# Batch 1's scores from interleaved queries, with its transposes inside batch 0's chain and batch 0's values loaded and transposed earlier

## The chip, the cores and the metric

The kernel runs on one core of a Trainium2 chip. The metric is device time in microseconds (us) of one execution. The runs of the kernel before have a median of 314.97 us over 14 runs (lowest 314.67, highest 319.38). One further execution was recorded by the hardware profiler; it took 315.0 us, and the span that the profile describes is 313.2 us of it.

The engines are named as in the profile: PE is the matrix engine, PEld its weight loads, DVE the vector engine, ACT the scalar engine, POOL the GpSimd engine, SP the sync engine. [...]

## The reference

Two computations follow one another. The first is an attention with a local window and eight global positions (8 batches, 8 heads, 576 positions, 64 numbers a head):

```python
scores = scale * np.matmul(q, k.transpose(0, 1, 3, 2))
mask = np.abs(pos[:, None] - pos[None, :]) <= 32
mask = mask | is_global[:, None] | is_global[None, :]
scores = np.where(mask, scores, -1000000000.0)
attn = softmax(scores)
x = attn @ v                    # then heads side by side: [8, 576, 512]
```

The second mixes along positions and then along channels:

```python
h = np.maximum(x^T @ w_tok1, 0) @ w_tok2     # 576 -> 256 -> 576
u = x + h^T
out = u + np.maximum(u @ w_ch1, 0) @ w_ch2   # 512 -> 1536 -> 512
```

## The kernel before

**Tiles and stages.** A batch has 576 positions: four tiles of 128 and a last one of 64. Its eight heads are two groups (`hg`) of four. Its stages are these.

- Load. `load_qk` and `load_v` issue DMAs from POOL's queue. Queries and keys land with positions on the partitions; `Xk` and `Xq` (L239 to L249) are DVE transposes of 32x32 blocks that bring the head dimension to the partitions, into the staging buffers `kcs[hg]` and `qcs[hg]`. `Kc` and `Xc` (L257 to L265) copy from there into `kT` and `qT`, whose tiles carry the eight global positions beside each tile's own (interleaved). `globals_` and `globals_k` write the global columns.
- Values. `V = vsh[b % 2]` has eight chunks `c`. `load_v(b)` issues a DMA for each; `dup_v(b)`, an SP DMA, then fills partitions 32 to 127 of chunks 5 to 7 with a copy of chunks 2 to 4. Batch 0 is different: `load_v0` brings the values of its middle positions into `v16` with four DMAs, `Xv0` transposes them on DVE (two halves, L142), and `shift_v0` copies on DVE (L134) what `dup_v` copies elsewhere.
- Scores (`S_...`): for a head group and one of two parts, matmuls with 32 rows write up to 512 columns for each head into PSUM, and `S_exp` (L323) lets ACT write the exponentials to `e_all` (`e0` for batch 0). The mask is either a bias that extra matmuls add (`biasm`, L298), or a multiplication by `bandm` afterwards on DVE (`S_mask`, L342). `S_eg` (L348) collects the global rows.
- `OG` (L358, and `OGh` L590 for batch 0) is the output of the global rows. Its result is written into the first rows of `V` (L364, L368), and a function `rest` (L371) copies it to further chunks.
- `PV` (L390, L393) multiplies with the values, and `norm` (L401, L402) divides on DVE.
- `M1` and `M2` are the mixing along positions, `M3` a transpose, `M4` (L472) and `M5` (L498) the mixing along channels: `M4` of a batch is 12 units of four matmuls of 512 columns, `M5` 16 units of three.

**Order.** Everything is one program written out in order; there is no scheduler. Batches from 1 on run as a software pipeline, in the loop at L1024: while the matrix engine does `M4` and `M5` of batch b, the scores of batch b+2 and the output stage of batch b+1 are woven in by `merge`. The head of the program does not have that. From L829 on batch 0 runs alone as a chain, one head group after another: scores, `OGh`, `rfh`, `PVh`, `normh`, `M1h`, `M2h`, `M3h`, `M4h`. After it, in the loop's turn `b == 0`, an order written out by hand (L1034 to L1040) runs the scores of batch 1 (`T`), its `OG` and `PV`, the preparation of batch 2 (`x2`) and the `M4` units of batch 0 (`M[2]` to `M[11]`) together. `M1(1)` ends it, and `M5` of batch 0 with the scores of batch 2 follows.

**Batch 1's scores.** In the kernel before they go through `S_nat` (L291), as batch 0's do: queries are read from `qcs[hg]` in plain order, so a stretch of columns that holds global positions too is cut into pieces by `pieces`, and the global columns come from `gqT` with matmuls of 8 columns. All four tiles of head group 1 carry the bias; those of head group 0 are masked on DVE. A tile here is two heads (`rp`) of a group and part. From batch 2 on, `S_mm` (L280, L286) reads the interleaved `qT` instead, four heads together.

**Buffers.** The PSUM pools are: `pss`, two buffers of two banks; `psv`, one buffer of two banks; `psm`, two of one bank. Score tiles take `pss` (some of batch 0's take `psv`).

Of the kernel before, what the change touches and what calls it, by code (L numbers as in the profile page):

```python
# [17 lines left out]
P = 128  # L18
NT = 5
# [6 lines left out]
NC = 8  # L26
# [26 lines left out]
def kernel(  # L53
# [12 lines left out]
    nc = tc.nc  # L66
# [65 lines left out]
    def shift_v0():  # L132
        for p in (32, 64):
            nc.vector.tensor_copy(  # L134
                out=vsh[0][p + 32 : p + 64, NT:NC].rearrange("p c h x -> p c (h x)"),
                in_=vsh[0][p : p + 32, 2:NT].rearrange("p c h x -> p c (h x)"),
            )

    def Xv0():
        for half in range(2):  # L140
# [173 lines left out]

    def S_exp(b, hg, part, rp, ps):
# [37 lines left out]
    def OG(b, get):  # L353
# [16 lines left out]
        def rest():  # L370
            (nc.vector.tensor_copy if b > 1 else nc.scalar.copy)(  # L371
# [362 lines left out]
    def zero_e(e):  # L734
        zeros(e[:, :, 136:208])
        zeros(win(e[:, :, 408:440], EB, 3))
# [87 lines left out]
    load_v0((0, 1))  # L824
    gather(gk, k, 0, (1,))
    gather(gq, q, 0, (1,))
    load_v0((2, 3))
# [12 lines left out]
    zero_e(e_all)  # L840
# [25 lines left out]
    nc.vector.memset(vsh[0][32:64, NT:NC, :, 0:D], 0.0)  # L866
# [12 lines left out]
    Xq(0, 1)  # L879
    glob0(1)  # L880
    S_nat(0, 0, 1, 0, psv, True)
    S_nat(0, 0, 1, 1, pss, True)
    load_v(0, (0, 5, 6, 7), False)
# [10 lines left out]
    load_v(1, range(NC), False)  # L894
    dup_v(1)
    S_nat(0, 1, 0, 0, pss, True)
    S_nat(0, 1, 0, 1, psv, True)
    Xv0()
    shift_v0()
    nc.vector.memset(e0[:, 0:4, 200:208], 0.0)  # L900
    S_eg(0, 0)

# [11 lines left out]
    S_nat(0, 1, 1, 1, pss, True)  # L914
    rfh(0, og)
# [49 lines left out]
    M3e(0, 0, pu[:, 0], nc.scalar.copy)  # L965
    Xk(1, 0)
    M2e(1, 0, h1[:, 0], False)
# [9 lines left out]
    M4h(1, (0, 1), 0, 4)  # L977
    M4h(0, (2, 3), 0, 2)
# [3 lines left out]
    load_qk(2, (0,))  # L982
    load_wc2()
    load_qk(2, (1,))
    load_v(2)

    def S1(hg, part, rp):
        S_nat(1, hg, part, rp, pss, hg == 1)

    globals_k(1, nc.vector, 1)  # L990
    Kc(1, 0, nc.vector)
    globals_k(1, nc.vector, 0, slice(0, 1))
    Xq(1, 0)
    Xk(1, 1)
    Kc(1, 1, nc.vector)
    globals_k(1, nc.vector, 0, slice(1, 2))
    Xq(1, 1)
# [26 lines left out]
    for b in range(B):  # L1024
        D4, D5 = dense(b)
        if b == 0:
            T = lambda *a: S1(*a)
            M = [f for _, f in D4]
            og, *pv = [f for _, f in phase_og(1)]
            x2 = []  # L1030
            for hg in range(2):
                x2.append(lambda hg=hg: (Xk(2, hg), Kc(2, hg, nc.vector), globals_k(2, nc.vector, 0, slice(hg, hg + 1))))
                x2.append(lambda hg=hg: Xq(2, hg))
            for f in (  # L1034
                lambda: M2(0, 2, psv), lambda: T(0, 0, 0), M[2], lambda: T(0, 0, 1), M[3], lambda: T(0, 1, 0), lambda: T(0, 1, 1), M[4],
# [59 lines left out]
```

## Time and profile before

| | |
|---|---|
| profiled execution | 315.0 us |
| its span in the profile | 313.2 us |
| median of 14 runs | 314.97 us |
| PE busy | 297.1 us, 95% |
| DVE busy | 191.2 us, 61% |
| ACT busy | 158.8 us, 51% |
| POOL busy | 106.1 us, 34% |
| chain that ended last, by engine | PE 77%, DVE 12%, issue 3%, ACT 3%, POOL 2%, DMA 1% |

Places on the span, in us from its start: batch 0's first scores at 11.05; its first `OGh` at 21.28; its first `M4h` at 36.56; batch 1's first scores at 38.9; batch 1's `OG` at 53.96; `M1(1)` from 61.39 to 63.71; first `M5` of batch 0 at 63.55; `M4` of batch 1 at 79.79.

A busy share is an average over stages. Durations in a row of groups are means of one instruction. Times of PE are those of the record, and neighbouring matmuls overlap. "Idle before" tells how long the engine was idle before an instruction and, behind the arrow, what ended the wait; "issue" there means that the engine waited for nothing that the profile shows.

### The profile page before, as it was taken

The page shows a single profiled execution, that of the slowest core. Times are in us where ns is not written, and L with a number is a line of the kernel's source. Part 1 is how long each engine was busy: PE and PEld are TensorE (multiplying, and loading weights), DVE is VectorE, ACT ScalarE, POOL GpSimd, SP SyncE. Part 2 cuts the span into 40 slices and gives each one's busy share as a digit, 9 for nine tenths or more (in the row PEclk, how much of TensorE's full clock was granted, in tenths as well). Part 3 has the DMA queues.
Part 4 walks back from the last instruction along what each step waited for, and adds up shares of the span by engine and source line. Part 5 has one row for each costly group of instructions (what it writes and reads, how often), then busy time and mean ns, then how long its engine had stood idle before and what let it go on. Part 6 is the DMA issues. An engine that isn't in the chain of part 4 may idle for free.

```text
span 313.2 us, 8382 instructions
## 1 busy us (share of the span) xinstructions
PE 297.1 (95%) x3507; PEld 161.8 (52%) x3507; DVE 191.2 (61%) x368; ACT 158.8 (51%) x321; POOL 106.1 (34%) x203
## 2 busy tenths in 40 slices
PE   8979897899989999999999999999999999999994
PEld 3668674544456445544466446444565446444641
DVE  8966785867556685947573867776582866240021
ACT  8964596666335454465446535563546625205500
POOL 7995282300688074217412371408030000000000
PEclk9998999999999999999999999999999999999999
DMA  7999999917699799628990499329601720061022
GB/s 108 129 120 195 194 143 222 154 42 150 130 143 159 134 126 150 161 47 122 137 183 0 70 143 209 86 70 135 132 2 16 154 69 2 0 167 50 3 86 82
DMA packets 69494, 34.66 MB, mean 111 GB/s; under 512 B 55984, under 2 KB 59952, under 8 KB 69456
## 3 DMA queue, kind: packets, MB, share of 16 engines
q0 software_dynamic: 44960, 18.19, 49.8%
q1 hardware_dynamic: 24496, 15.94, 20.5%
q8 instruction: 27, 0.44, 0.6%
q14 instruction: 11, 0.09, 0.1%
HBM read 36.38 MB, written 9.44 MB: 146 GB/s over the span
## 4 chain that ended last, share of the span: by engine, by line
PE 77%; DVE 12%; issue 3%; ACT 3%; POOL 2%; DMA 1%; DVEq 0%; ACTq 0%
PE b1p L472 25%; PE op L498 23%; PE a1p L415 5%; DVE e_all L342 5%; PE hp L431 4%; PE s L286 4%; PE b1lp L485 3%; PE pv L390 3%; PE s L309 2%; PE pv L393 2%; DMA v<-in_v_dram 1%; PE og L358 1%; DVE osb L502 1%; ACT e_all L323 1%; DVE u L436 1%
## 5 line engine op out<-in xcount | busy, mean ns | idle before, releaser
L699 ACT ACTIVATE big<-b1p 128x512 f16<-128x512 f32 x96 | 57.2, 598 | 79.3 <-PE b1p L472 78.0
L472 PE MATMUL b1p<-uT,wc 128*128 128x512 f16 x376 | 91.9, 379 | 2.6 <-DVE osb L502 1.5
L498 PE MATMUL op<-big 128*128 128x512 f16 x384 | 91.8, 380 | 0.0
L323 ACT ACTIVATE e_all<-s 128x544 f16<-128x544 f32 (+3 forms) x140 | 58.8, 515 | 34.1 <-PE s L286 30.8
L498 PEld LDWEIGHTS <-big 128*128 128x128 f16 x384 | 35.5, 98 | 40.5
L472 PEld LDWEIGHTS <-wc 128*128 128x128 f16 x376 | 33.3, 97 | 39.3 <-issue 6.5
L125 POOL DMA_DIRECT2D vsh<-in_v_dram x60 | 41.8, 709 | 20.4 <-DMA wc<-in_moe_w_ch_dram 5.4
L342 DVE TENSOR_TENSOR e_all<-e_all,bandm 128x1160 f16<-128x1160 f16 x52 | 36.7, 757 | 14.6 <-ACT e_all L323 14.6
L502 DVE TENSOR_TENSOR osb<-u,op 128x512 f32<-128x512 f16 x32 | 21.9, 684 | 24.3 <-PE op L498 24.0
L436 DVE TENSOR_TENSOR u<-x,hp 128x1024 f16<-128x1024 f16 x14 | 17.1, 1218 | 30.6 <-PE hp L431 30.6
L348 POOL COPY eg<-e_all 128x160 f16<-128x160 f16 (+1 forms) x24 | 6.4, 295 | 77.9 <-DVE e_all L342 77.9
L402 DVE TENSOR_TENSOR x<-pv,rr 128x512 f16<-128x512 f32 (+1 forms) x35 | 24.2, 691 | 1.3
L253 POOL COPY kT<-kc 128x640 int32<-128x640 int32 x11 | 8.1, 733 | 40.5 <-DVE rr L401 35.0
L390 PEld LDWEIGHTS <-e_all 128*128 128x128 f16 (+1 forms) x280 | 18.1, 98 | 6.4 <-issue 2.0
L390 PE MATMUL pv<-vsh,e_all 128*128 128x66 f16 (+1 forms) x280 | 20.3, 193 | 0.2 <-DVE x L402 0.2
L431 PE MATMUL hp<-a,w 128*128 128x512 f16 x72 | 19.1, 379 | 0.9 <-DVE u L436 0.9
L240 DVE STREAM_TRANSPOSE kc<-k 128x576 int32<-128x576 int32 x16 | 19.9, 1242 | 0.1
L246 DVE STREAM_TRANSPOSE qc<-q 128x576 int32<-128x576 int32 x16 | 19.8, 1239 | 0.0
L393 PE MATMUL pv<-vsh,e_all 128*128 128x66 f16 x224 | 17.2, 193 | 0.6 <-DVE vsh L368 0.6
L286 PEld LDWEIGHTS <-kT 32*128 32x128 f16 x768 | 11.9, 92 | 10.7 <-issue 9.9
L364 DVE TENSOR_TENSOR vsh<-og,dsel 32x132 f16<-32x132 f32 x28 | 8.1, 289 | 13.7 <-PE og L358 13.3
L393 PEld LDWEIGHTS <-e_all 128*128 128x128 f16 x224 | 14.6, 97 | 3.1
(161 smaller groups left out, 339.3 us busy)
## 6 DMA issues: line engine op xcount, KB each, us to landing
out_dram<-osb SPq DMA_DIRECT2D x32, 256.0 KB, 2.3
k<-in_k_dram POOLq DMA_DIRECT2D x16, 288.0 KB
q<-in_q_dram POOLq DMA_DIRECT2D x16, 288.0 KB
vsh<-in_v_dram POOLq DMA_DIRECT2D x36, 96.0 KB
vsh<-vsh SPq DMA_DIRECT2D x7, 297.0 KB, 5.7
wc<-in_moe_w_ch_dram POOLq DMA_DIRECT2D x3, 512.0 KB
big<-in_moe_w_ch_dram POOLq DMA_DIRECT2D x3, 512.0 KB
out_dram<-osb SPq DMA_DIRECT2D x8, 128.0 KB, 7.8
```

Source lines behind the costliest of these rows:

```text
L125: nc.gpsimd.dma_start(out=V[p0:p1, c, :, 0:D], in_=v[b, :, j0 : j0 + p1 - p0, :].rearrange("h p d -> p h d"))
L286: nc.tensor.matmul(tiles[r // 2][:, r % 2, off : off + n], lhsT=kT[rs, kc : kc + P, e], rhs=qf[rs, lo : lo + n, e], start=(e == 0), stop=( ...
L323: nc.scalar.activation(out=o, in_=i, func=AF.Exp, scale=scale)
L342: nc.vector.tensor_mul(out=eh, in0=eh, in1=bandm)
L390: nc.tensor.matmul(o[0:m], lhsT=e[:, h, c0 : c0 + m], rhs=vs[:, tau, h, :], start=True, stop=(tau == NT - 1))
L393: nc.tensor.matmul(o, lhsT=e[:, h, c1 : c1 + P], rhs=vs[:, NT - 1 + tau if tau else 1, h, :], start=False, stop=True)
L402: nc.vector.tensor_tensor(out=x16[r, tau, :].rearrange("p (f h x) -> p f h x", f=2, h=4), in0=pq[r, :, :, 0:D], in1=rr[r].unsqueeze(3).to_ ...
L431: nc.tensor.matmul(ps[:, i, :], lhsT=w2[:, ch, P * tau - sh : P * tau - sh + P], rhs=s["a1"][:, ch, :], start=(ch == 0), stop=(ch == 1),)
L472: nc.tensor.matmul(ps, lhsT=wc1[:, cc, P * j : P * j + P], rhs=s["uT"][:, :, cc, :], start=(cc == 0), stop=(cc == 3))
L498: nc.tensor.matmul(ps, lhsT=w, rhs=wc2[:, j, :], start=(j == 0), stop=(j == NJ - 1))
L502: nc.vector.tensor_add(out=osb, in0=s["u16"][:, tau], in1=ps)
L699: nc.scalar.activation(out=st[b]["b1"][:, j, :], in_=ps, func=AF.Relu)
```

## The change

**Values of batch 0.** All four `load_v0` DMAs are issued before the two gathers of head group 1 (before: two ahead of them and two behind), and `load_v(0, (0,))` directly after these, ahead of POOL's copy `Kc(0, 1)`. `Xv0` is split into its two halves, which stand around `glob0(1)` on DVE, ahead of six score tiles; before, both stood behind these, just ahead of `shift_v0`. The memset of a part of `vsh[0]` moves from DVE to ACT. The zeroing of `e_all`, which stood there on ACT, moves behind batch 0's last score tile.

**Batch 1's keys and queries.** `Xq(1, 0)` joins `Xk(1, 0)` inside batch 0's chain, and the four transposes of batch 1 are all ahead of its first score tile. `Kc(1, ...)` goes from DVE to POOL. `Xc(1, ...)`, which did not exist for batch 1, is added on POOL. `globals_(1)` (which did not exist either) and `globals_k(1, ..., 1)` run on DVE at about the place of batch 0's first `S_eg`.

**Batch 1's scores.** A new function `S_tile` takes the place of `S_nat`: the same tile of two heads, read from `qT` in uncut stretches. Only two of the eight tiles keep the bias (`hg == 1 and rp == 1`), and `S_mask(1, 1, (0, 1))` is added on DVE. The first tile is issued between batch 0's `M4h` groups.

**Values of batch 1.** The loads are issued in another order, in between other work on POOL. `dup_v(1)` is replaced by the DVE copies (`shift_v(1)`) and a memset on POOL. `rest` of batch 1 goes from ACT to DVE.

**Preparation of batch 2.** Its `Kc` and `Xc` go to POOL (before: `Kc` twice and `Xc` once on DVE, `Xc` once on ACT). `load_v(2)` is split: three chunks at the old place, and five with `dup_v(2)` at the end of the written-out order.

The diff, cut to its core:

```diff
-    def shift_v0():
+    def shift_v(b):
...
-    def Xv0():
-        for half in range(2):
+    def Xv0(half):
+        if True:
...
+    def S_tile(b, hg, part, rp, bias):
+        ps = pss([P, 2, 512], name=f"s_{b}_{hg}_{part}_{rp}")
+        qf, kT = q16s[b % 2][:, hg], k16s[b % 2][:, hg]
+        if bias:
+            for i in range(2):
+                for off, c0, n in B_SEG[part]:
+                    nc.tensor.matmul(
+                        ps[:, i, off : off + n], lhsT=identS, rhs=biasm[:, c0 : c0 + n], start=(off == 0), stop=False,
+                    )
+        for off, kc, lo, n in S_SEG[part]:
+            for e in range(2):
+                for i in range(2):
+                    r = 2 * rp + i
+                    rs = slice(32 * r, 32 * r + 32)
+                    nc.tensor.matmul(
+                        ps[:, i, off : off + n], lhsT=kT[rs, kc : kc + P, e], rhs=qf[rs, lo : lo + n, e],
+                        start=(e == 0 and not bias), stop=(e == 1 and (off == S_SEG[part][-1][0] or not bias)),
+                    )
+        S_exp(b, hg, part, rp, ps)
...
         def rest():
-            (nc.vector.tensor_copy if b > 1 else nc.scalar.copy)(
+            nc.vector.tensor_copy(
...
-    load_v0((0, 1))
+    load_v0((0, 1, 2, 3))
     gather(gk, k, 0, (1,))
     gather(gq, q, 0, (1,))
-    load_v0((2, 3))
+    load_v(0, (0,), False)
...
-    zero_e(e_all)
+    zeros(vsh[0][32:64, NT:NC, :, 0:D])
...
-    nc.vector.memset(vsh[0][32:64, NT:NC, :, 0:D], 0.0)
     glob0(0)
...
     Xq(0, 1)
+    Xv0(0)
     glob0(1)
+    Xv0(1)
     S_nat(0, 0, 1, 0, psv, True)
     S_nat(0, 0, 1, 1, pss, True)
-    load_v(0, (0, 5, 6, 7), False)
+    load_v(0, (5, 6, 7), False)
...
     eg_const(1, nc.gpsimd.tensor_copy)
-    load_v(1, range(NC), False)
-    dup_v(1)
+    nc.gpsimd.memset(vsh[1][32:64, NT:NC, :, 0:D], 0.0)
+    load_v(1, (2, 3, 4), False)
     S_nat(0, 1, 0, 0, pss, True)
     S_nat(0, 1, 0, 1, psv, True)
-    Xv0()
-    shift_v0()
+    shift_v(0)
     nc.vector.memset(e0[:, 0:4, 200:208], 0.0)
     S_eg(0, 0)
+    globals_(1, nc.vector)
+    globals_k(1, nc.vector, 1)
...
     S_nat(0, 1, 1, 1, pss, True)
+    zero_e(e_all)
     rfh(0, og)
...
     M3e(0, 0, pu[:, 0], nc.scalar.copy)
+    load_v(1, range(1), False)
     Xk(1, 0)
+    Kc(1, 0, nc.gpsimd)
+    Xq(1, 0)
+    Xc(1, 0, nc.gpsimd)
+    load_v(1, range(1, 2), False)
     M2e(1, 0, h1[:, 0], False)
...
     M4h(1, (0, 1), 0, 4)
+    globals_k(1, nc.vector, 0, slice(0, 1))
+    Xk(1, 1)
+    Kc(1, 1, nc.gpsimd)
+    Xq(1, 1)
+    Xc(1, 1, nc.gpsimd)
+    globals_k(1, nc.vector, 0, slice(1, 2))
+    load_v(1, range(5, 8), False)
+    load_qk(2, (0,))
+    load_wc2()
+    load_qk(2, (1,))
+    load_v(2, range(3), False)
+
+    def S1(hg, part, rp):
+        S_tile(1, hg, part, rp, hg == 1 and rp == 1)
+
+    S1(0, 0, 0)
     M4h(0, (2, 3), 0, 2)
...
-    load_qk(2, (0,))
-    load_wc2()
-    load_qk(2, (1,))
-    load_v(2)
-
-    def S1(hg, part, rp):
-        S_nat(1, hg, part, rp, pss, hg == 1)
-
-    globals_k(1, nc.vector, 1)
-    Kc(1, 0, nc.vector)
-    globals_k(1, nc.vector, 0, slice(0, 1))
-    Xq(1, 0)
-    Xk(1, 1)
-    Kc(1, 1, nc.vector)
-    globals_k(1, nc.vector, 0, slice(1, 2))
-    Xq(1, 1)
...
-            og, *pv = [f for _, f in phase_og(1)]
+            _, *pv = [f for _, f in phase_og(1)]
+            og = lambda: OG(1, pss)()
             x2 = []
+            gk2 = [lambda hg=hg: globals_k(2, nc.vector, 0, slice(hg, hg + 1)) for hg in range(2)]
             for hg in range(2):
-                x2.append(lambda hg=hg: (Xk(2, hg), Kc(2, hg, nc.vector), globals_k(2, nc.vector, 0, slice(hg, hg + 1))))
-                x2.append(lambda hg=hg: Xq(2, hg))
+                x2.append(lambda hg=hg: (Xk(2, hg), Kc(2, hg, nc.gpsimd)))
+                x2.append(lambda hg=hg: (Xq(2, hg), Xc(2, hg, nc.gpsimd)))
             for f in (
-                lambda: M2(0, 2, psv), lambda: T(0, 0, 0), M[2], lambda: T(0, 0, 1), M[3], lambda: T(0, 1, 0), lambda: T(0, 1, 1), M[4],
-                lambda: T(1, 0, 0), lambda: S_mask(1, 0, (0, 1)), lambda: T(1, 0, 1), lambda: S_mask(1, 0, (2, 3)), lambda: S_eg(1, 0),
-                M[5], lambda: T(1, 1, 0), lambda: globals_k(2, nc.vector, 1), x2[0], lambda: T(1, 1, 1), M[6], lambda: nc.vector.memset(e_all[:, 4:8, 200:208], 0.0),
-                lambda: S_eg(1, 1), x2[1], M[7], og, M[8], pv[0], lambda: globals_(2, nc.vector), pv[1], M[9], pv[2], pv[3], M[10], pv[4], lambda: Xc(2, 0, nc.scalar), x2[2], M[11],
-                lambda: M1(1, pss), x2[3], lambda: Xc(2, 1, nc.vector),
+                lambda: T(0, 0, 1), lambda: M2(0, 2, psv), M[2], lambda: T(0, 1, 0), M[3], lambda: T(0, 1, 1),
+                lambda: S_mask(1, 0, (0, 1)), lambda: T(1, 0, 0), lambda: S_mask(1, 0, (2, 3)), lambda: S_eg(1, 0), M[4],
+                lambda: T(1, 0, 1), lambda: T(1, 1, 0), M[5], lambda: T(1, 1, 1), lambda: shift_v(1), lambda: S_mask(1, 1, (0, 1)),
+                lambda: nc.vector.memset(e_all[:, 6:8, 200:208], 0.0), lambda: S_eg(1, 1), lambda: globals_k(2, nc.vector, 1), M[6], M[7], x2[0], og, M[8], M[9], pv[0], pv[1],
+                lambda: globals_(2, nc.vector), pv[2], x2[1], M[10], pv[3], pv[4], M[11], lambda: M1(1, pss), gk2[0],
+                x2[2], x2[3], gk2[1], lambda: load_v(2, range(3, 8)),
             ):
                 run(f)
```

## The prediction

> **What bounds the kernel now.** I read the page's first part, then the stretches of ten microseconds, then the chain of waits of the head, then PE's timeline and the groups by shape. The page, and the table of stretches (busy time and count of each engine, TensorE clock, DMA share, GB/s):
>
> ```profile
> PE 297.1 (95%) x3507; PEld 161.8 (52%) x3507; DVE 191.2 (61%) x368; ACT 158.8 (51%) x321; POOL 106.1 (34%) x203
> ```
>
> ```profile
> 10.00:20.00 10.00, 8.83 (x258) 7.35 (x256) 7.80 (x19) 9.51 (x20) 9.35 (x15) 1.00 0.93 98
> 20.00:30.00 10.00, 8.36 (x217) 7.13 (x218) 6.74 (x22) 5.09 (x12) 7.34 (x12) 0.83 1.13 177
> 30.00:40.00 10.00, 8.89 (x111) 6.53 (x108) 7.72 (x14) 5.22 (x10) 3.11 (x5) 1.00 1.49 193
> 40.00:50.00 10.00, 9.86 (x254) 7.02 (x253) 8.41 (x20) 9.13 (x22) 6.95 (x11) 1.00 1.24 173
> 50.00:60.00 10.00, 7.59 (x140) 4.85 (x140) 6.00 (x18) 4.90 (x8) 3.08 (x5) 1.00 1.46 195
> 100.00:110.00 10.00, 10.00 (x135) 4.86 (x133) 5.07 (x7) 5.01 (x12) 1.19 (x4) 1.00 0.82 154
> ```
>
> From about 64 us on PE is full; the change leaves that alone. It works on the head, where no engine is full throughout: ACT is at 9.1 of 10 from 40 to 50, PE loses 2.4 from 50 to 60, the clock is down from 20 to 30. So what was late in each part decides. The chain of waits, head (start, length, what):
>
> ```profile
> 13.24 4.20 DMA v<-in_v_dram
> ...
> 17.52 2.13 DVE vsh L142 x2
> ...
> 19.68 0.56 DVE vsh L134
> ...
> 21.28 0.43 PE og L590 x25
> ...
> 49.86 1.70 issue
> ...
> 55.90 0.30 DVE vsh L368
> ```
>
> Batch 0's values set the time of its first `OGh`: DMA, transpose, shift. Much later PE stands still for 1.70 in the middle of a score tile, waiting for nothing that the record names. PE's timeline at the two gaps, and ACT in between (its idle time before):
>
> ```profile
> 21.28 0.43 PE L590 MATMUL og<-vsh,eg 128*32 128x66 f16 x32 [1.83 <-DVE eg L348]
> ```
>
> ```profile
> 49.12 1.03 ACT L323 ACTIVATE e_all<-s 128x544 f16<-128x544 f32 x2 [0.45 <-PE s L309]
> 52.24 1.03 ACT L323 ACTIVATE e_all<-s 128x544 f16<-128x544 f32 x2 [2.09 <-PE s L309]
> ```
>
> Last, POOL's timeline where it waits for a free place in its DMA queue, which tells when earlier loads landed, and PE's row of a four-head score step:
>
> ```profile
> 30.87 0.77 POOL L125 DMA_DIRECT2D vsh<-in_v_dram x1 [1.59 <-DMA wc<-in_moe_w_ch_dram]
> ...
> 57.87 0.58 POOL L125 DMA_DIRECT2D vsh<-in_v_dram x1 [0.83 <-DMA k<-in_k_dram]
> 59.63 0.58 POOL L125 DMA_DIRECT2D vsh<-in_v_dram x1 [1.18 <-DMA q<-in_q_dram]
> ```
>
> ```profile
> 68.43 0.62 PE L286 MATMUL s<-qT,kT 32*128 32x136 f16 x32
> ```
>
> [...] an instruction block of 16 KB is among the DMA packets from 49.3 to 50.2, where the stall begins (49.86), with the data queues full (DMA share 1.24). [...] Here 0.83 over ten microseconds is 3.4 us at half, right after the 1.83 gap. [...] POOL copies of 0.72 to 0.75 from 97.6 to 100.9 stand beside transposes of 1.19 that are no longer than others (1.25); beside DVE copies no run here shows them.
>
> **Part by part.**
>
> *1. Values of batch 0.* The third and fourth `load_v0` move past two gathers on POOL (1.02 + 0.99 + two pauses of 0.30): issued by 11.3 instead of 13.88, landing near 17.44 - 2.6 = 14.8. DVE is 0.91 early (memset 0.70 and its pause 0.21 gone), so `Xq(0,1)` ends near 14.45. `Xv0(0)` 14.8 to 15.9. The gathers go 1.26 later, the query one from 12.66 to 13.9; before, its data were there at 15.64 without a wait; I take 16.0. `glob0(1)`, 0.63, to 16.6; `Xv0(1)` to 17.7; two shifts, 1.14, to 18.9; `S_eg` to 19.3. `OGh` at 19.4 or, with pauses, 19.7 instead of 21.28: 1.6 (0.5 if the gather lands at 17). `Kc(0,1)` goes 0.7 later, to 15.5, hidden: its reader starts after 16.8. ACT's 1.40 of zeroing is replaced by one of 1536 columns, near 1.45 by the slope of its rows (576 in 0.67, 768 in 0.83).
>
> The gap on PE falls from 1.83 to some 0.6, and with it the reason of the half clock. What that cost: a biased tile 1.96 instead of 1.22 (by the chain's rows), 32 `PVh` matmuls 1.7 instead of 1.0 (the second group); 1.4 in all. I count 0.8 (0 to 1.4). `zero_e` (1.40) falls into ACT's 1.24 pause ahead of `rfh(1)`: -0.2. DVE's new `Xq(1,0)`, 1.25, fits its pause of 1.65 ahead of L669, if the queries have landed (POOL's waits put that at 28.5, it starts at 30.4); without that cover it costs 1.25. Sum at the first `M4h`: **2.2**, 34.4 instead of 36.56.
>
> *2. Batch 1's scores.* PE: an unbiased tile by `S_nat` takes 0.75 (36 matmuls), by `S_tile` 16. The nearest row is the four-head step L286, 32 matmuls in 0.62: 0.31 if two heads cost half, 0.75 if nothing is won; I take 0.5, eight times 0.25 = 2.0 (0 to 3.5). Two biases less, 0.9. The program has 158 matmuls and as many weight loads fewer here, more than a block of 256, so the 1.70 stall should go (0 to 1.9).
>
> But ACT then decides. Its exponentials of a tile take 1.16 (three, part 0) or 1.03 (two, part 1) in its timeline, 4 x 1.16 + 4 x 1.03 = 8.8; an `M4` eviction in a row takes 0.54 (two in 1.08), and six fall in between, 3.25: 12.05 from the first exponential to the last. Before: 39.68 to 53.27, 13.6. It starts at 34.4 + 0.87 (two `M4h` groups) + 0.5 = 35.8 and ends at 47.9, or 48.1 with pauses: 5.2 earlier, so **3.0** of this part's own. What must be ready: `Kc`, `Xc(1,0)` on POOL wait behind a `load_v` whose ring is free at 30.87, so 31.6 to 33.2; group 1 near 37.4, used from 40. DVE: minus 1.64 of copies, plus `S_mask` 1.44 and `shift_v(1)` 1.14: about 6 us of work between 38 and 48, hidden by ACT. The values it shifts land by 42, as the DMA queues have the same bytes.
>
> *3. `OG` to `M1(1)`.* Before, 53.96 to 63.7. Now DVE stands in line: from the end of `S_eg` at 48.5, globals 0.18, `Xk(2,0)` 1.25, OG's five 1.5, `rest` 0.96 (before on ACT, 1.51), five norms 4.5, `globals_` 0.26, `Xq(2,0)` 1.25: 9.9, then `M1`'s last matmuls 0.45: 58.9, against 63.7: 4.8 in all, so this part gives back **-0.4**. PE's work between (`OG` 0.6, four `M4` 3.9, five `PV` 2.2, `M1` 2.2) is 8.9, below it, and hides `OG`'s DVE part behind `M[8]` and `M[9]`, which stand ahead of the first `PV` now.
>
> *4. Behind it.* `Xk`, `Xq(2,1)` wait for their data (POOL's waits: 57.9, 59.6) and end near 61; the next DVE user, `M2(1,0)`'s addition (67.89 before), comes at 63; without that cover what is late next is `M2(1,1)`, as `psv` has one buffer. Removing `dup_v(1)` frees nothing on SP that was late. The five late loads of batch 2's values follow on POOL, land near 66.5, and `dup_v(2)` is ahead of the DMA transposes on SP: the first, wanted at 69.14 - 4.9 = 64.2, waits until 67; the second, wanted at 69.3, goes at 69.9 and lands 3.9 later, 73.8; `M4(1)` reads it at 74.9. Hidden by 1.1; **-0.1**.
>
> Sum 2.2 + 3.0 - 0.4 - 0.1 = **4.7**. The profiled execution took 315.0 (span 313.2 and 1.8 around it), the median is 314.97: **310.3**.
>
> **Rivals.**
> *A, half.* The head gains 1.0 at most (late gather, clock still halved) and instruction blocks still come late, since the DMA queues stay full (share 1.2 to 1.5 from 30 to 60): 2.3, 312.7. For it: which block is late depends on transfers.
> *B, DVE is the bound.* Removed from it 0.70 + 4 x 0.82 + 0.82 = 4.8, added 1.44 + 1.14 + 0.96 = 3.5: 1.3, 313.7. Against it: DVE is idle 13 of the 50 us from 10 to 60, 4.0 of them at 50 to 60.
> *C, slower[...].* Eight POOL copies of 0.75 to 0.83 and a memset of some 0.7 hold off DVE's copies or wait for them, each on the path: up to 7.3 - 4.7 = 2.6, 317.6. It decides above 0.6 us a copy on the path. Against it: most stand beside transposes and PSUM reads.
> That the tiles aren't faster on PE costs little: ACT decides.
>
> **From cases to numbers.** Forecast 0.62 (own range 308.8 to 312.0), A 0.17, B 0.12, C 0.09. 0.5% is 1.6 us, about what a measurement of this kernel can tell from no change: under 313.4 is faster, 0.79; same 0.12; slower 0.09. Below 308.6 (clock, stall and tiles all at their best) I leave 0.06, above 314.2 C and a little of B: range 308.6 to 314.2.
>
> **What would show it.** `OGh` near 19.7 and no half clock at 20 to 30; first `M4h` near 34.4; score rows of some 0.5 a tile and no stall above 1 us on PE near 45 to 50; batch 1's `OG` near 48.5 and the end of `M1(1)` near 59; `M4` of batch 1 at 75, with the same distance to the end as before. Wrong if DVE copies beside POOL's grow by more than 0.5, if SP's transposes land after 75, or if the DMA landings of batch 2's keys hold DVE past 63.

## The result and the profile after

The kernel after took 312.98 us (median of 10 runs, 309.60 to 313.97); the kernel before, in 47 runs beside it, 315.48 (314.47 to 319.38). The ratio is 0.9878, 95% interval [0.9846, 0.991]: faster by 1.2%. The forecast of 310.3 is 2.7 too low: within the whole range (308.6 to 314.2), but outside the part of it that the forecast's own steps were given (308.8 to 312.0). Medians and ranges here and below take in every execution, ratios and their intervals leave out those more than 1.5% above their kernel's fastest. With the profiled one and one more, twelve executions of the kernel after have a recorded mean TensorE clock: the four at 0.996 or more took 309.60 to 310.26, the eight at 0.971 to 0.989 took 312.16 to 313.97.

The profiled execution took 312.16 (span 310.4, mean clock 0.989). Its page, engine shares, and the same stretches of ten microseconds as before (busy time and count of PE, PEld, DVE, ACT, POOL; TensorE clock, DMA share, GB/s):

```profile
PE 296.6 (96%) x3349; PEld 160.3 (52%) x3349; DVE 190.1 (61%) x369; ACT 157.0 (51%) x320; POOL 113.2 (36%) x212
```

```profile
10.00:20.00 10.00, 9.36 (x255) 7.50 (x255) 8.65 (x22) 8.75 (x18) 9.35 (x15) 1.00 0.97 105
20.00:30.00 10.00, 8.35 (x204) 6.85 (x197) 5.47 (x21) 6.70 (x15) 8.81 (x14) 0.71 1.14 183
30.00:40.00 10.00, 8.89 (x110) 6.96 (x109) 7.89 (x15) 4.75 (x9) 3.64 (x5) 0.95 1.55 187
40.00:50.00 10.00, 10.00 (x153) 6.26 (x151) 7.12 (x18) 10.00 (x25) 9.14 (x14) 1.00 0.84 107
50.00:60.00 10.00, 9.67 (x135) 5.38 (x133) 9.57 (x26) 4.13 (x8) 1.44 (x2) 1.00 1.31 200
```

Two things are to be seen. From 40 to 60 the change does what it was said to do: PE is full at 40 to 50, and 2.1 us fuller at 50 to 60 (7.59 before). From 20 to 30 it is worse than before: the clock is 0.71 (0.83 before), although the pause of 1.83 ahead of `OGh`, on which the half clock had been blamed, is gone. PE's timeline (start, length, what; idle time before):

```profile
20.41 0.42 PE L610 MATMUL og<-vsh,eg 128*32 128x66 f16 x32 [0.15 <-DVE eg L368]
...
23.48 0.18 PE L309 MATMUL s<-gqT,kT 32*128 32x8 f16 x2 [1.50 <-issue]
...
38.03 1.02 PE L711 MATMUL b1p<-uT,wc 128*128 128x512 f16 x4
38.99 0.64 PE L329 MATMUL s<-qT,kT 32*128 32x136 f16 x16
...
51.25 0.64 PE L378 MATMUL og<-vsh,eg 128*32 128x132 f16 x32
```

The `OGh` at 20.41 waits 0.15 instead of 1.83. But in the next score tile PE stands still for 1.50 us, waiting for nothing that the record names: the kind of stall that stood at 49.86 before is gone there and has appeared here. Then the clock is half from 24.21 to 31.04 (before: 22.93 to 26.35), and the first `M4h` starts 1.5 later than before, not 2.2 earlier. What the head lost, the next part more than won back. By places:

| | before | forecast | after | kernel f1 below |
|---|---|---|---|---|
| first `OGh` | 21.28 | 19.7 | 20.41 | 20.04 |
| first `M4h` | 36.56 | 34.4 | 38.03 | 34.49 |
| from the first `M4h` to `OG` of batch 1 | 17.40 | 14.1 | 13.22 | 13.21 |
| from that `OG` to `M4` of batch 1 | 25.83 | 26.3 | 25.84 | 25.99 |
| from that `M4` to the end of the span | 233.4 | 233.4 | 233.3 | 233.3 |

(The forecast column follows from its steps: 48.5 - 34.4, and 25.83 + 0.4 + 0.1.) Everything behind `M4` of batch 1 is as long as before; the change acts in the head alone.

### The profile page after: what moved, and what is told of

It reads as the page before. It is cut to its first block, busy times and chain, and to the rows that moved or that the text cites. A ratio compares the mean times of both kernels' runs of the same rounds, so it can differ in the third digit from the quotient of the medians.

```text
span 310.4 us, 8076 instructions
## 1 busy us (share of the span) xinstructions
PE 296.6 (96%) x3349; PEld 160.3 (52%) x3349; DVE 190.1 (61%) x369; ACT 157.0 (51%) x320; POOL 113.2 (36%) x212
## 4 chain that ended last, share of the span: by engine, by line
PE 68%; DVE 7%; issue 2%; ACT 1%; DVEq 0%; ACTq 0%
PE op L518 24%; PE b1p L492 23%; DVE e_all L362 5%; PE hp L451 4%; PE a1p L435 4%; PE s L286 4%; PE b1lp L505 3%; PE pv L410 2%; PE pv L413 2%; DVE osb L522 1%; ACT e_all L343 1%; PE og L378 1%; DVE u L456 1%; DVE osb L525 0%; ACT big L719 0%
## 5 line engine op out<-in xcount | busy, mean ns | idle before, releaser
L362 DVE TENSOR_TENSOR e_all<-e_all,bandm 128x1160 f16<-128x1160 f16 x54 | 38.2, 758 | 15.7 <-ACT e_all L343 15.7
L253 POOL COPY kT<-kc 128x640 int32<-128x640 int32 x15 | 10.9, 725 | 51.4 <-DVE rr L421 35.0
```

The costliest lines, as they stand in the source:

```text
L362: nc.vector.tensor_mul(out=eh, in0=eh, in1=bandm)
```

## Experiments

Two theories. **T1:** both parts work as forecast, but in most executions the first part's gain is eaten by a half clock in the head and by an instruction block that comes late. **T2**, the rival: the first part has no 2 us to give (the gather, the DMA queues and POOL's copies beside DVE's work take them), and the whole gain is the second part's. Kernels named with the same letter ran on one chip, beside the kernel before (h alone on another). On these chips the kernel before has medians from 314.76 to 317.54, so medians are compared within a letter. The places named are those of each kernel's one profiled execution.

**e1: only batch 0's values.** The kernel before with this, cut to its core:

```diff
-    load_v0((0, 1))
+    load_v0((0, 1, 2, 3))
...
-    load_v0((2, 3))
+    load_v(0, (0,), False)
...
-    zero_e(e_all)
+    zeros(vsh[0][32:64, NT:NC, :, 0:D])
...
-    nc.vector.memset(vsh[0][32:64, NT:NC, :, 0:D], 0.0)
...
+    Xv0(0)
     glob0(1)
+    Xv0(1)
```

> The kernel before with the changes to batch 0's values alone (all four value loads ahead of the gathers, transposes around the second head group's globals, memset moved to ACT, zeroing of the exponentials moved back). Theory 1 (the value path is shortened, but a late instruction block on PE and the halved clock behind it take the gain): the first OGh comes near 20.4 instead of 21.28, PE stands still for 1 to 2 us near 21.8 to 23.5 in the score tile behind it, and the first M4h is not earlier than 36.5; time within 1 us of before, 314 to 316. Rival (the value path itself gains nothing, because the gathers come later): OGh after 21.0 and no stall behind it; time 315. As forecast in step 1: first M4h at 34.4, time 312.8.

317.18 (22 runs, 312.92 to 323.38) against 315.96 (33 runs): ratio 0.999 [0.9956, 1.0023], no change clear of noise. In the profiled execution the clock is half from 15.90 to 29.55, so the first `OGh` is at 22.39 and the first `M4h` at 38.81. Theory 1 had expected `OGh` near 20.4 and a stall behind it; neither came, since the clock fell before, among the first score tiles. Twelve of the 22 executions have a mean clock of 0.978 or less (10 of the 33 of the kernel before); the one at 0.999 is the fastest, 312.92. A null on the median, and a first hint for T1 as to the clock; as to the late block it shows nothing.

**e2: everything but that.** The kernel after with the edits of e1 taken back.

> The changed kernel with batch 0's values as they were before, so only batch 1's scores, queries, copies, values and the preparation of batch 2 are changed. Theory 1: the first OGh is at 21.3 and the first M4h at 36.5 to 36.8 as before; from there to the end of M1(1) 22.8 us as in the changed kernel (27.1 before), so the end of M1(1) near 59.5 and a time of 311. Rival (the two parts need one another: the gain in the scores is only room that the earlier values made): 313.5 or more.

312.47 (6 runs, 310.13 to 314.25), ratio 0.9899 [0.9844, 0.9955]: the second part alone gives nearly all of the gain. Here no stall and no half clock fell into the head, and `OGh` waits 1.55 again (21.24); the first `M4h` is at 35.81, `OG` 13.20 later. From the first `M4h` to the end of `M1(1)` it takes 22.97, as expected (22.8); the time of 311 was missed, since only two of the six executions have a clock of 0.997 or more.

**e3: the old form of tile.** The kernel after with its queries read in plain order again, 144 matmuls more, biases as in the kernel after:

```diff
-        S_tile(1, hg, part, rp, hg == 1 and rp == 1)
+        S_nat(1, hg, part, rp, pss, hg == 1 and rp == 1)
```

> The changed kernel with batch 1's score tiles by the old function, cut at the global columns, in the same order and with the same two biased tiles: 144 matmuls more. Theory 1 (ACT decides in this stage, and the shorter tiles matter through the number of instructions): without a stall of PE from 36 to 52 the stage is at most 0.5 longer, and the time 0 to 0.7 above the changed kernel's; with a stall at a multiple of 256 instructions it is 1.5 to 2 longer. Rival (the shorter tiles are the gain): eight tiles by 0.2 to 0.25, 1.6 to 2.0 more, with no stall in PE's timeline.

312.93 (6 runs, 311.04 to 317.69), ratio 0.9882 [0.9829, 0.9935]. Its profiled execution is of more use than the median, since here neither stall nor half clock stands ahead of the first `M4h`. PE's timeline:

```profile
19.89 0.43 PE L610 MATMUL og<-vsh,eg 128*32 128x66 f16 x32
...
34.79 1.02 PE L711 MATMUL b1p<-uT,wc 128*128 128x512 f16 x4
...
48.92 0.18 PE L309 MATMUL s<-gqT,kT 32*128 32x8 f16 x1 [1.76 <-issue]
...
49.23 2.94 PE L492 MATMUL b1p<-uT,wc 128*128 128x512 f16 x8
```

`OGh` at 19.89 and the first `M4h` at 34.79: 1.8 earlier than before and 1.0 earlier than in e2, so the values do move the head when nothing else falls into it. And with the matmuls back the stall is back at the old place in batch 1's tiles; from the first `M4h` to `OG` it takes 17.31, 4.1 more than in e2. That is more than the stall: a half clock follows it, from 49.94 to 53.35, in which the two `M4` units ahead of `OG` take 2.94 instead of 1.90. With 1.76 for the stall and 1.04 for the clock, some 1.3 is left for the cut tiles themselves (an estimate from these figures). Theory 1 allowed them at most 0.5, the rival 1.6 to 2.0; the measured value lies between, nearer to the rival.

**e4: a border moved.** Counting PE's records in the order of the trace (matmuls, weight loads, and the few semaphore waits and the drain among them), the stall of the kernel before lies behind number 1729, that of the kernel after behind 705, that of e3 behind 1729 again: each number is 193 more than a multiple of 256. The DMA records hold as many packets of 16 KB on the queue that they name instruction (q8) as there are such numbers: 27 in the kernel before (7051 records), 26 in the kernel after (6737). If the stall belongs to a block of 256 instructions, then it moves with the block's border and not with the work. So the 33 idle matmuls of 512 columns at the start were cut into 66 of 256, the same time in 66 instructions more:

```diff
-    fillt(psm([P, 512], name="w"), FILL[0])
+    wps = psm([P, 512], name="w")
+    for _ in range(2 * FILL[0]):
+        nc.tensor.matmul(wps[:, 0:256], lhsT=zz[:, 0:P], rhs=zz[:, 0:256], start=True, stop=True)
```

> The changed kernel with each of the 33 warm-up matmuls of 512 columns as two of 256 columns: the same columns on PE, 66 instructions more ahead of everything, so that every border of 256 instructions falls 66 instructions earlier in the program [...]. Theory 1 (a late block of instructions stalls PE at 21.8): the stall moves or goes; if it goes, the clock stays up or is down for one window at most, the first M4h comes at 34.5 to 36 instead of 38.0, and the median is near 310. Rival (the stall at 21.8 is a wait on data or on a semaphore): it stays at the same matmul of the same score tile, and the time is unchanged at 312 to 314.

313.78 (12 runs, 312.31 to 314.04), ratio 0.9932 [0.9902, 0.9962]: not better. The stall is gone from 705 and stands behind number 961, the next border, which is now in the middle of the second `OGh`:

```profile
27.16 0.46 PE L610 MATMUL og<-vsh,eg 128*32 128x66 f16 x18 [2.64 <-issue]
```

So it is a matter of blocks. Nor is the block there sooner: its packet starts at 24.88, 4.6 behind PE's crossing of the border ahead (20.32). Whether a block is late because of the DMA queues is the question of the next run.

**f1: later weight loads.** POOL's memset and constant copy, 2.1 us, moved ahead of the weight loads:

```diff
     load_v(0, (5, 6, 7), False)
+    nc.gpsimd.memset(vsh[1][32:64, NT:NC, :, 0:D], 0.0)
+    eg_const(1, nc.gpsimd.tensor_copy)
     nc.gpsimd.dma_start(out=w1, in_=moe_w_tok1[0 : S - LAST, :].rearrange("(c p) x -> p c x", p=P))
...
-    eg_const(1, nc.gpsimd.tensor_copy)
-    nc.gpsimd.memset(vsh[1][32:64, NT:NC, :, 0:D], 0.0)
     load_v(1, (2, 3, 4), False)
```

> The kernel after, with POOL's memset and its constant copy (1.37 and 0.75 in its timeline) moved ahead of the weight loads, so that these and batch 1's loads are issued some 2.1 us later, at 19.2 instead of 17.04. Theory (a late instruction block took step 1's gain): in the kernel after, the block that PE needs at instruction 705 is among the packets only at 21.08, 2.64 behind PE's crossing of the border before it (18.44), since these loads had filled the DMA queues from 17.0 on; with the queues emptier its packet comes within some 1.2 of the crossing, PE doesn't stand still at 21.78, and the first M4h is near 35 to 36 instead of 38.03 (what a half clock costs apart). The time falls to 310 to 312. Rival (the stall has nothing to do with the queues): it stays, at the same instruction, with 1.5 to 1.7 us, and the time is 312 to 314, as the kernel after's.

Its executions took 308.82 and 309.56 (mean clock 0.999) and 312.89 to 313.10 (four, 0.974 to 0.976); median 312.89, ratio 0.9844 [0.9773, 0.9914]. The profiled one is that of 308.82. Its PE timeline, at the places of the table:

```profile
20.04 0.43 PE L610 MATMUL og<-vsh,eg 128*32 128x66 f16 x32
...
34.49 1.02 PE L711 MATMUL b1p<-uT,wc 128*128 128x512 f16 x4
...
47.70 0.64 PE L378 MATMUL og<-vsh,eg 128*32 128x132 f16 x32
```

No stall at a border, no half clock, and the first `M4h` at 34.49, where the forecast had 34.4. The DMA view shows the block. The border ahead of number 705 is number 449; PE crosses it at 18.44 in the kernel after and at 18.23 in f1. DMA packets of the kernel after from 18.4 to 21.0, and then from 21.0 to 22.5 (queue, packets, MB, share of 16 engines):

```profile
q0 software_dynamic: 763, 0.34, 115.9%
```

```profile
q0 software_dynamic: 175, 0.19, 102.2%
q8 instruction: 1, 0.02, 4.0%
```

and of f1 from 18.2 to 19.5:

```profile
q0 software_dynamic: 63, 0.01, 8.8%
q8 instruction: 1, 0.02, 4.5%
```

With the data queues at 115.9% no instruction packet starts for 2.6 us (at 21.08, by the packet's own record; done at 22.04); with them at 8.8% it starts 0.2 us behind the crossing (18.46). Two more readings of the traces support this. There are nine pauses at such numbers, of 0.33 to 2.64 us, in the kernel before, the kernel after, e1, e3, e4 and h; in each, PE goes on 1.30 to 1.53 us behind the end of a block's packet. And it depends on what is in the queues: the weight loads' own packets begin near 18.6 in the kernel after and in e3, which has the same head. e3 crosses at 18.14, just ahead of them, has its packet at 18.17 and no stall; the kernel after, e1, f2, f3, f4 and g0 cross from 18.44 to 20.32 and have it from 20.50 to 21.29. That the stall goes with a late packet is shown; its price on the median isn't, for f2, which has the loads at the old place, is as fast in its executions at full clock (309.15, 309.31).

**f2: three idle matmuls ahead of the first `M1h`**, where PE waits for DVE (`FILL = (33, 2, 0, 3)` instead of `(33, 2, 0, 0)`).

> The kernel after, with three idle matmuls of 512 columns more, ahead of the first M1h, where PE waits for DVE (0.69 and 0.24 in the run that had no stall); they add 6 instructions and put the border of a block elsewhere by 6. Theory (the half clock is set off by PE's gaps in the head): the clock is up in more of the executions, their mean clock is 0.99 or more, and the median is 310 to 311.5. Rival (it is not such gaps, but what PE did in the windows before, or when they fall): mean clocks scatter from 0.97 to 0.998 as in the kernel after, and the median is 312 to 313.8.

312.98 (6 runs), clocks of 0.971 to 0.975 in four and 0.999 to 1.0 in two: the rival was right, this is not the place. The half clock of its profiled execution begins at 15.29, long before these matmuls.

**f3: the copies on DVE.** `Kc` and `Xc` of batches 1 and 2, eight in all, with `nc.vector` for `nc.gpsimd`.

> The kernel after, with its eight copies of keys and queries (Kc and Xc of batches 1 and 2) on DVE instead of POOL. Theory (POOL takes them off DVE's line[...]): DVE has eight copies of some 0.4 more, 3.3 us, of which four at the head stand in the line from the transposes to batch 1's second group of tiles and four in the line from OG to M1(1), where DVE decides; 1 to 2.5 us slower than the kernel after, 313.5 to 315. Rival C [...]: equal or faster, 311 to 313, and DVE's copies of globals and of the band are back at 0.25 and 0.46 from 0.64 and 0.87.

316.60 (22 runs, 312.46 to 319.84), ratio to the kernel before 0.995 [0.9915, 0.9985]: at like clocks the copies on DVE cost 3.3 (312.46 against f2's 309.15, clocks 1.0 and 0.999) or some 3 (316.17 at 0.975 against 312.9 to 313.3 of f1 and f2). More than the theory's 1 to 2.5: a copy takes 0.82 on DVE, not the 0.4 that the expectation used, and PE now waits for DVE at both places. DVE's and PE's timelines of f3:

```profile
35.25 0.82 DVE L255 COPY kT<-kc 128x1280 f16<-128x1280 f16 x1
```

```profile
38.74 0.40 PE L696 MATMUL pu<-ident,u 128*128 128x128 f16 x4 [1.70 <-DVE u L689]
...
64.68 0.59 PE L435 MATMUL a1p<-x,w 128*128 128x512 f16 x2 [0.79 <-DVE x L422]
```

Rival C falls. POOL's copies do cost DVE something: beside one its band takes 0.87 in the kernel after, and 0.47 in f3. But that lies off the path: ahead of the first instruction that reads the band DVE waits 1.88 for ACT.

**f4: all four biases back**, and without the mask multiplication that stood for two of them (`S_tile(1, hg, part, rp, hg == 1)`).

> The kernel after, with the bias matmuls in all four tiles of head group 1 of batch 1 (as before) and without the mask multiplication on DVE that stood for two of them; 32 instructions more, so that borders of blocks fall on other instructions. Theory (ACT decides in this stretch): PE has 0.9 more and some of it lies beside ACT's exponentials, DVE has 0.7 less; OG of batch 1 is 0.0 to 0.6 later, counted from the first M4h (13.2 in the kernel after), and the median is within 0.6 of the kernel after's, apart from what the block and the clock do. Rival (PE decides): 0.9 later, counted in the same way.

314.72 (6 runs, 310.44 to 315.22), 1.8 above f1 and f2; from the first `M4h` to `OG` it takes 14.47, 1.25 more. The rival was right, and with 0.9 somewhat low. ACT's timeline shows it: where in the kernel after ACT runs through, it now waits for PE.

```profile
49.29 2.10 ACT L343 ACTIVATE e_all<-s 128x544 f16<-128x544 f32 x5 [0.34 <-PE s L329]
51.32 0.60 ACT L719 ACTIVATE big<-b1p 128x512 f16<-128x512 f32 x1
52.28 1.03 ACT L343 ACTIVATE e_all<-s 128x544 f16<-128x544 f32 x2 [0.37 <-PE s L329]
```

**The half clock.** Seven of the profiled executions so far have one in the head. Each lasts 3.42 or a multiple of it (6.83, 13.65, 17.07), and so do the stretches at full clock around them in the clock's record: 17.07 and 286.72 in the kernel before, 17.07 and 279.89 in the kernel after, which are 5, 84, 5 and 82 times 3.413. So in these traces the clock changes at the edges of windows of 3.41 us. The edges, taken modulo 3.41, differ from execution to execution (2.45 in the kernel before, 0.32 in the kernel after). PE was idle throughout none of the windows ahead of one of these half clocks. PE's busy time (first number after the length) in the window ahead of a half clock, in the kernel before, in e1 and in f4:

```profile
19.52:22.93 3.41, 1.65 (x72) 1.42 (x73) 2.72 (x10) 1.24 (x3) 3.41 (x7) 1.00 1.10 138
```

```profile
12.48:15.90 3.42, 3.03 (x102) 2.45 (x96) 3.42 (x6) 2.32 (x5) 3.13 (x4) 1.00 0.82 110
```

```profile
11.30:14.71 3.41, 2.36 (x80) 2.06 (x80) 3.37 (x8) 2.41 (x3) 3.00 (x3) 1.00 0.81 144
```

The first holds the pause ahead of `OGh` (the kernel after: its stall of 1.50, 1.91 busy). The others hold the first score tiles: many matmuls of 8 columns and 32 rows, with a pause of 0.39 and 0.50 that ends near 14.18 among them. Busy time alone doesn't decide, since f1 kept its clock with less than e1 had:

```profile
13.05:16.47 3.42, 2.90 (x87) 2.44 (x85) 3.32 (x9) 2.29 (x6) 3.38 (x5) 1.00 0.90 94
```

The traces hold a better measure. Count for every matmul its columns, times the share of the array that it uses (a score matmul has 32 of 128 rows and counts a quarter, one of 128x128 counts in full), and add these up over each trace's windows, a matmul in the window where it starts. A window full of idle 128x128 matmuls has 8192 (the kernel after, from 7.14). Over all 14 traces the eleven windows that a half clock follows, apart from the end of the program, have at most 3048 (e1's; f4's 2048, that of the kernel before 2344). The 1193 windows at full clock that none follows have at least 3072 (that of f1 shown above has 3392), even one in which PE is busy for 1.57 us alone (the kernel after, from 304.1). So the work done in the array parts the two without an exception, with the edge between 3048 and 3072 of 8192, and busy time doesn't. The same measure fits how long the clock stays half: of the 30 windows at half clock the 19 that another one follows have 3055 or less, the 11 that end it 2969 or more, though PE is busy throughout nearly all of them. This was read from the traces afterwards, and no run was made to test the edge.

The pause ahead of `OGh` is therefore not enough by itself: in e2 (1.55) and in h (1.66) an edge falls into it, the windows on both sides have 3072 to 3236, and the clock stays up. A window with more work of the whole array in it should stay above the edge.

**g0, g1, g2: denser windows.** g0 is the kernel after, unchanged. g1 is f1 with three idle matmuls between the biases and the products of the first tile:

```diff
     def S_nat(b, hg, part, rp, get, bias):
...
+        if b == hg == part == rp == 0:
+            fillt(psm([P, 512], name="w"), 3)
         for off, kc, lo, n in S_SEG[part]:
```

g2 is g1 with two more ahead of the second tile and two ahead of the third.

> The kernel after, unchanged, beside the next two on the same chip. Theory: its executions fall into those with a mean clock of 0.996 or more, near 309.7, and those at 0.97 to 0.99, from 312 to 314; the median is where the greater part lies.

> The kernel with POOL's memset and constant copy ahead of the weight loads, and three idle matmuls of 512 columns between the biases and the products of the first score tile, where PE waits 0.4 to 0.7 for the first global queries. Theory (the half clock comes when PE's work in one window of 3.4 us is too thin, and the windows from 11.3 to 16.3 are on the edge: 0.58 to 0.75 of PE's time in the four profiled executions whose clock fell there): this window gains some 0.1, more executions keep the clock, mean clocks of 0.996 or more in at least half of them, median 309 to 311. Rival (three matmuls are too little, or thin is not what matters): clocks and median as without them, 312 to 313.5 with 0.975.

> The kernel of the run before, with two idle matmuls more ahead of the second score tile and two ahead of the third, 0.9 us of PE. They add 0.2 to 0.9 us to the head, as far as PE decides there. Theory: no execution has a half clock in the head, mean clock 0.997 or more in nearly all, 309.3 to 310.2. Rival: the clock scatters as before, 313 to 314.

| | median | runs | mean clocks | ratio to before, same chip |
|---|---|---|---|---|
| g0 | 309.27 | 307.90 to 312.89 (8) | 0.970 to 1.0, two below 0.98 | 0.9801 [0.9756, 0.9847] |
| g1 | 308.30 | 307.61 to 313.52 (6) | 0.969 to 1.0, two below 0.98 | 0.9776 [0.972, 0.9832] |
| g2 | 307.82 | 307.29 to 310.58 (6) | 0.996 to 1.0 | 0.9785 [0.9735, 0.9835] |

g0's theory failed: its executions don't fall into the two groups of the first chip. One has its clock at 1.0, five lie at 0.986 to 0.992 and took 308.08 to 309.77, and only the two below 0.98 (311.77 and 312.89) come near the slow group; so the long half clock was rarer on this chip. The medians of g1 and g2 lie below what was expected, 309 to 311 and 309.3 to 310.2. g1's clocks did what its theory said (four of six at 0.996 or more), though the expectation's 0.58 to 0.75 of PE's time doesn't fit the four windows it means: by the view used above PE is busy for 0.69 to 0.89 of them. In g2 all six kept their clock. PE is full in both windows that were at the edge (g2), and no window of its head has less than 3884 by the measure above:

```profile
8.61:12.02 3.41, 3.41 (x27) 1.69 (x27) 2.60 (x13) 3.34 (x7) 3.11 (x6) 1.00 1.12 146
12.02:15.44 3.42, 3.42 (x94) 2.64 (x95) 3.42 (x6) 3.33 (x6) 3.07 (x5) 1.00 0.76 123
```

and the 1.5 us of idle matmuls cost nothing in its head (with three of them, in g1, `OGh` still waits 0.40 for DVE): first `OGh` 20.07, first `M4h` 34.52, as in f1. g2's median is 1.45 below g0's on the same chip; at full clock the two are level (307.90 for g0, 307.29 to 307.93 for five of g2), so what the idle matmuls bring is the clock. f1 wasn't run on this chip, so its later weight loads may have a share in it. g2's slowest execution, 310.58 at a clock of 0.999, isn't explained. The intervals of the ratios overlap, so that it beats the kernel after is not settled, though its highest run is below g0's two slowest.

**h: the same seven idle matmuls in the kernel before.**

> The kernel before, with the seven idle matmuls of 512 columns of the run before this one (three between biases and products of the first score tile, two ahead of the second, two ahead of the third), and nothing else. Theory (its half clock comes from the pause of 1.83 ahead of the first OGh, which these don't touch, and the change takes that pause away): the long half clock in the head (mean clocks of 0.965 to 0.98) becomes rare, the short one (0.985 to 0.99) stays, and the median is 313.8 to 315.2, under the kernel before by 0.5 to 1.5 on the same chip. Rival (the idle matmuls alone bring what they bring in the kernel after): all clocks at 0.996 or more, 312.5 or less.

314.44 (14 runs, 313.74 to 316.29) against 314.76 (19 runs): ratio 0.9989 [0.9959, 1.0018]. None of the 14 executions has a clock of 0.978 or less, 5 of the 19 of the kernel before have; so the long half clock became rare, as expected; the median didn't fall by the 0.5 to 1.5 of the theory. In the profiled execution the pause ahead of `OGh` stays:

```profile
21.92 0.43 PE L592 MATMUL og<-vsh,eg 128*32 128x66 f16 x32 [1.66 <-DVE eg L350]
```

But no half clock follows it, so the theory's cause isn't what this execution shows. The first `M4h` is at 36.33, 0.2 earlier than before, and then a half clock stands from 51.64 to 55.05, behind a late block (a pause of 1.56, number 1729): from the first `M4h` to `OG` it takes 18.80 instead of 17.40. So the idle matmuls bring nothing that the median shows by themselves; that they pay only together with the early values fits g2, and isn't shown by a pair of runs on one chip.

## Why the prediction was right, and where it was wrong

**Step 1, the values, failed on its second half.** Forecast 2.2; in the profiled execution it was -1.5. The arithmetic of the first half stood: `OGh` with hardly a wait (0.15), and in f1, with clock and blocks undisturbed, the first `M4h` at 34.49 against a forecast of 34.4. It was late by 0.3 to 0.7 at `OGh`, as the first gather, not the one named, was: DVE waited 0.93 for it, which took the 0.91 that the memset had freed. The timeline of DVE in the kernel after:

```profile
11.92 0.21 DVE L218 STREAM_TRANSPOSE gkT<-gk 128x32 int32<-128x32 int32 x1 [0.93 <-DMA gk<-in_k_dram,idx_i]
```

The sentence that failed is "the gap on PE falls from 1.83 to some 0.6, and with it the reason of the half clock". The gap fell further, to 0.15, and the half clock came all the same, in 8 of 12 executions: the stretch of the first score tiles is thin enough by itself (3048 in e1), and in the profiled execution the stall of 1.50 made another window thin (2268). The price of one window at half was sized well: e2, with `OGh` as late as before (21.24) and its clock up, has the first `M4h` 0.75 earlier than the kernel before, against the 0.8 that was counted (an estimate, since e2 differs there in more than the clock). But a long half clock costs 3.3 to 4.3 us (f1's 308.82 and 309.56 against 312.89 to 313.10), which the range of 0 to 1.4 did not hold. e1 shows the step whole on the median: nothing.

**And it had counted a late block once.** The step took the stall away at 49.86 and put none elsewhere. The pause ahead of `OGh` had been cover: in the kernel before, PE crossed the border at 17.63, the packet started at 18.76, and PE came to the end of its block at 22.65, 5.0 us behind the crossing. Without the pause it comes there 3.3 us behind the crossing (18.44 and 21.77 in the kernel after). And there the crossing is later, since the first tiles are, and falls behind the weight loads that POOL issues from 17.04 on. The prediction asked of each wait what else it was hiding, but not of this one. The block of 256 that step 2 counted with is what the traces show (e4, and the 27 packets for 7051 records). Nor does every border cost something: the kernel before passes 26 of its 27 without a pause of PE, the kernel after 25 of its 26; at the nine crossings with one PE stands still for 0.33 to 2.64 us.

**Step 2, batch 1's scores, was right and too small.** Forecast 3.0, measured 4.2 (17.40 to 13.22, the same in e2 and f1). The tile of 0.5 was right: rows of 0.64 and 0.61 for 16 matmuls, two tiles in 1.00. That the stall would go with some 158 matmuls was right (e3: with 144 back, it is back). Of the 4.2, 1.7 is the stall, 1.25 the two biases (f4) and some 1.3 the uncut tiles (the estimate of e3). The mis-sized term is ACT's 12.05, a sum of rows: neighbouring activations overlap, and from the first exponential (39.67) to the end of the last (50.65) it took 11.0. The timeline of ACT, two tiles in a row:

```profile
44.68 2.09 ACT L343 ACTIVATE e_all<-s 128x544 f16<-128x544 f32 x5
```

against 1.16 + 1.03 by the single rows. "ACT then decides" was only half of it: PE is busy 13.27 of the 13.30 us from 38.0 to 51.3, the two are level, and f4 shows that the two biases less, counted as hidden, are worth 1.25.

**Step 3** (-0.4) and **step 4** (-0.1): 25.83 before, 25.84 after, nothing. DVE does stand in line there nearly without a pause, but the work summed as 9.9 takes it 9.4 in f1 (47.5 to 56.9): again rows that overlap. SP's second transpose went out at 71.45, which is 5.64 ahead of `M4` of batch 1, just as before (74.15 and 79.79), where the forecast had 5.0: `M4` didn't wait for it.

**The sum.** -1.5 + 4.2 + 0 = 2.7 in the profiled execution, which took 2.8 less than the one of before (312.16 against 315.0). In f1's it is 2.1 + 4.2 - 0.2 = 6.1, and 308.82. So with the clock up and no late block the two parts together were worth more than the forecast's 4.7. The median shows less, because most executions of the kernel after have a half clock in the head, many a longer one than the single window that the forecast had priced. (The kernel before always has some: none of the 33, 27, 11 and 19 executions beside the runs exceeds 0.995.) That 312.98 lies inside the range is in part luck: the 1.2 that step 2 gave beyond its forecast stands against the 3.7 that step 1 lost in the profiled execution.

**The rivals.** A, "half", is the nearest to what the median shows (312.7): clock still halved, a block still late because the queues are full, though it put the late block into the wrong part of the kernel and a late gather at the wrong gather. B, DVE as the bound, wasn't it: it is 9.57 of 10 busy from 50 to 60, but `M1(1)` ends 9.8 behind `OG`, as before. C fell with f3.

**Open.** Whether the work done in the array is what the clock's window counts: it parts all windows of these traces, but the edge between 3048 and 3072 rests on few windows near it, and no run was aimed at it. What the short pause is that ends at 14.14 to 14.19 in eight of the profiled executions, at different instructions. And how often the kernel after has its stall behind 705: one profiled execution shows it; f2 and g0, with the same order there, have their clock down already and take 5.0 from crossing to border, so that their late packet is still in time.

## What to carry to other kernels

A pause may be the cover of something that the profile doesn't name, here an instruction block behind full DMA queues (2.6 us late at 116%) and a clock on its edge (3048 against 3072): before counting its removal as gain, look at what arrives during it. If runs of one kernel fall into groups, read the granted clock of each first, and look at the stretch in which it falls: here not PE's busy time but the share of the array in use parted the windows that lost the clock from those that kept it, and matmuls of 32 rows left it thin (3048 of 8192 in e1, with PE busy for 3.03 of 3.42 us). Idle matmuls of the whole array, in a place where the matrix engine waits anyway, cost nothing here (g2: first `M4h` at 34.52, f1's at 34.49). Where two engines are level, work that one of them does is not hidden by the other (the two biases, 1.25 here), and a sum of rows overstates a chain of overlapping activations (12.05 against 11.0 here).

## What the runs showed of the hardware

- A stall of PE that no semaphore explains lay, in six kernels and nine times, behind a number of PE's records that is 193 more than a multiple of 256 (705, 961, 1473, 1729, 1985), and moved with the count of instructions (e4). PE went on 1.30 to 1.53 us behind the end of the block's packet of 16 KB. There were 27 such packets for 7051 records (the kernel before) and 26 for 6737 (the kernel after). The packet of the block at 705 started 0.2 us (f1) and 1.1 us (the kernel before) behind the crossing of the border ahead of it, and 2.6 us behind in the kernel after, with the data queues at 116%.
- The clock was halved after windows of 3.41 us in which the columns of the matmuls, each times its share of the 128x128 array, came to 2048 to 3048 of 8192, and never after one of 3072 or more (11 and 1193 windows of the 14 traces). PE was busy for 1.40 (f3) to 3.03 us (e1) in the eleven. It stayed half for up to five windows although PE was busy throughout (f4: 14.71 to 31.78).
- A copy of 128x640 words on POOL (0.72) stretched DVE's band of 1160 columns from 0.47 to 0.87, while DVE's transposes beside such copies in the kernel after stayed at 1.22 and 1.23 (1.25 without one), and a norm that reads PSUM at 0.69 (at 58.71; 0.69 without one).
